# Halving the columns of the down projection's matmuls in the last eight tiles, and issuing them in runs of four

## The chip, the cores and the metric

The kernel runs on one core of a Trainium2 chip. The metric is the device time of one execution in microseconds (us), as the median over several runs. Engines are named as the profile names them: PE is TensorE's matmuls, PEld its weight loads, DVE VectorE, ACT ScalarE, POOL GpSimd, SP the queue that issues the DMAs.

## The reference

Two blocks follow each other. The first is a long convolution over the sequence, done with Fourier transforms. The second is an expert layer with a cosine gate, on each of the 49,920 rows that the first one gives. The change touches the second alone.

```python
# first block: x, v are (4, 12480, 128)
u = x * v
y = irfft(rfft(u, 2*S) * rfft(h_filt, 2*S))[:S]     # along the sequence
x2 = (x * y).reshape(49920, 128)
# second block: w_in (128, 2048), w_out (2048, 128)
h = x2 @ w_in
g = h * cos(h)
out = g @ w_out                                     # (49920, 128), float32
```

All is float32, in and out.

## The kernel before

The convolution is cut into steps that are mixed into the expert layer's loop for as long as there are any. Its last matmuls (line 504) start at 2945.7 us of the profiled execution; after that the expert layer runs alone. The prediction is about this last part.

**Tiles.** The 49,920 rows are taken four to a partition row: `G = 4`, so there are 12,480 groups of four. They form `NALL = 98` tiles: tile 0 with 104 groups (416 columns), tiles 1 to 96 with 128 (512 columns), tile 97 with 88 (352 columns). `NFC = 16` slices of 128 hidden features make the 16 steps of a tile. The loop over `steps` (lines 947 to 974) goes through all pairs of tile and slice; the variable `i` counts them.

**One step.** `moe_up` (740) multiplies a slice of `w_in` with the tile's rows into a bank `ph` of PSUM (PE, line 743). Then a chain of four engines forms h·cos(h). ACT scales `ph` and adds a quarter turn into `a` (746), DVE rounds `a` to `k` (749), POOL takes the difference `f` (752). `moe_act` (755) lets ACT take the sine of `f` into `cs` (757), and DVE multiplies it with `ph` into `gt` (759). `moe_down` (762) multiplies `gt` with a slice of `w_out` and sums it up over the 16 slices in one bank of PSUM, named `acc` for even tiles and `cv` for odd ones (PE, line 768).

**Order.** The engines run what they are given in the order in which the program gives it. In round `i` the loop issues the up projection of step `i` with its `a`, `k` and `f`, then the down projection of step `i - 4` (`LAG = 4`), after a tile's sixteenth down projection `moe_evict` (ACT, 774, the sums copied from PSUM into `ot`), and then `moe_act` of step `i - 1`, that is `cs` and `gt`. So on ACT the `cs` of one step stands behind the `a` of the next. After that come two visits of PE per tile that are transposes: `moe_turn` after the tile's step 3 turns the next tile's rows (four transposes at line 126, copied by ACT into `at` at 737), and `moe_back` at step 8 turns the finished sums of the tile before (four transposes, copied by ACT into `ob` at 783). `moe_store` (786) sends `ob` out by DMA.

**Banks.** `ph` is a ring of four PSUM banks (`ps_h`, line 910). `moe_up`, `moe_turn` and `moe_back` each take the next one, and it is free again when the last reader of its former content is done: `gt` for an up projection, the copies `at` and `ob` for the transposes. `a` has three buffers, `k`, `f` and `cs` two each, `gt` four, `ot` and `ob` one each.

**`slots`** (line 807) is the large SBUF tile of the convolution, 128 partitions of 64 x 240 x 2 values. It is not used after the convolution's end.

Of the kernel before, what the change touches and what calls it, by code (L numbers as in the profile page):

```python
# [9 lines left out]
F32 = mybir.dt.float32  # L10
# [6 lines left out]
P = 128  # L17
BANK = 512
# [12 lines left out]
def kernel(  # L31
# [46 lines left out]
    nc = tc.nc  # L78

    B, S, D = x.shape  # L80
    FO = pos_emb.shape[1]
    DFF = moe_w_in.shape[1]
    N1, N2 = 96, 120
# [15 lines left out]
    NFC = DFF // P  # L99
    G = BANK // D  # L100
    UA = 2
    NG = N2 // G
    NROWS = B * NG * R
    NALL = 1 + math.ceil((NROWS - R) / P)
    assert G == 2 * UA and H % UA == 0 and N2 % G == 0
    LAG = 4
    WCOL = 256

    dram = ctx.enter_context(tc.tile_pool(name="dram", bufs=1, space=DRAM))
# [14 lines left out]
    def transpose(dst, src, ident):  # L124
        n = src.shape[0]
        nc.tensor.transpose(dst, src, ident[0:n, 0:n])  # L126


    def float32_parts(pool, raw):
        lo, hi = raw[:, :, 0], raw[:, :, 1]  # L130

        power = pool.tile([P, WCOL], U32, name="power", bufs=2)
        nc.vector.tensor_scalar(out=power[:, :], in0=hi, scalar1=20, scalar2=0x7FF,
# [5 lines left out]

        sig = pool.tile([P, WCOL], U32, name="sig", bufs=2)  # L140
        nc.vector.tensor_scalar(out=sig[:, :], in0=hi, scalar1=0xFFFFF, scalar2=0x100000,
                                op0=ALU.bitwise_and, op1=ALU.bitwise_or)
        high = sig[:, :].bitcast(F32)
        nc.scalar.activation(high, sig[:, :], AF.Copy, scale=2.0 ** -20)
        low = pool.tile([P, WCOL], F32, name="low", bufs=1)
        nc.scalar.activation(low[:, :], lo, AF.Copy, scale=2.0 ** -52)
# [3 lines left out]
    def float32_join(dst, raw, power, high):  # L150
# [6 lines left out]
        if dst.space == DRAM:  # L157
# [3 lines left out]
    out_words = moe_w_out.bitcast(U32).rearrange("(c p) (q w) -> p c q w", p=P, w=2)  # L161
    in_pieces = [(slice(c, c + WCOL), in_words[:, c:c + WCOL, :])
                 for c in range(0, DFF, WCOL)]
    out_pieces = [(slice(c, c + WCOL // D), out_words[:, c:c + WCOL // D, :, :])
                  for c in range(0, NFC, WCOL // D)]
# [106 lines left out]
    def third_table(pool):  # L272

        return pool.tile([N2, 2, N2], F32, name="cs")
# [249 lines left out]
    made = [0]  # L524
# [191 lines left out]
    ats, accs = {}, {}  # L716

    def first_row(n):
        return min(R + (n - 1) * P, NROWS) if n else 0

    def rows_of(n):
        return first_row(n + 1) - first_row(n)
# [7 lines left out]
    def moe_turn(pool, n):  # L730
        m = rows_of(n)
        zb = zbs.pop(n)
        pt = ps_h.tile([P, BANK], F32, name="ph")
        for i in range(G):
            transpose(pt[:, i * m:(i + 1) * m], zb[0:m, i, :], ident)
        at = pool.tile([D, BANK], F32, name="at")
        nc.scalar.copy(out=at[:, 0:G * m], in_=pt[:, 0:G * m])
        ats[n] = at

    def moe_up(pool, n, c):  # L740
        m = G * rows_of(n)
        ph = ps_h.tile([P, BANK], F32, name="ph")
        nc.tensor.matmul(ph[:, 0:m], w_in_sb[:, c * P:(c + 1) * P], ats[n][:, 0:m],  # L743
                         start=True, stop=True)
        a = pool.tile([P, BANK], F32, name="a", bufs=3)
        nc.scalar.activation(a[:, 0:m], ph[:, 0:m], AF.Identity,  # L746
                             bias=quarter[:, 0:1], scale=INV_TWO_PI)
        k = pool.tile([P, BANK], F32, name="k")
        nc.vector.tensor_scalar(out=k[:, 0:m], in0=a[:, 0:m], scalar1=ROUND,  # L749
                                scalar2=ROUND, op0=ALU.add, op1=ALU.subtract)  # L750
        f = pool.tile([P, BANK], F32, name="f")
        nc.gpsimd.tensor_tensor(f[:, 0:m], a[:, 0:m], k[:, 0:m], op=ALU.subtract)  # L752
        return ph, f, m

    def moe_act(pool, ph, f, m):
        cs = pool.tile([P, BANK], F32, name="cs")
        nc.scalar.activation(cs[:, 0:m], f[:, 0:m], AF.Sin, scale=TWO_PI)  # L757
        gt = pool.tile([P, BANK], F32, name="gt", bufs=4)
        nc.vector.tensor_tensor(gt[:, 0:m], ph[:, 0:m], cs[:, 0:m], op=ALU.mult)  # L759
        return gt  # L760

    def moe_down(n, c, gt):
        if c == 0:

            accs[n] = bank() if made[0] == B * NG and n % 2 else \
                ps_acc.tile([P, BANK], F32, name="acc")
        m = G * rows_of(n)
        nc.tensor.matmul(accs[n][:, 0:m], w_out_sb[:, c, :], gt[:, 0:m],  # L768
                         start=(c == 0), stop=(c == NFC - 1))

    def moe_evict(pool, n):
        m = G * rows_of(n)
        ot = pool.tile([D, BANK], F32, name="ot", bufs=1)
        nc.scalar.copy(out=ot[:, 0:m], in_=accs.pop(n)[:, 0:m])
        return ot

    def moe_back(pool, n, ot):
        m = rows_of(n)
        pt = ps_h.tile([P, BANK], F32, name="ph")
        for i in range(G):  # L780
            transpose(pt[0:m, i * D:(i + 1) * D], ot[:, i * m:(i + 1) * m], ident)
        ob = pool.tile([P, 2, UA * D], F32, name="ob", bufs=1)
        nc.scalar.copy(out=ob[0:m, :, :].rearrange("p h n -> p (h n)"), in_=pt[0:m, :])
        return ob

    def moe_store(n, ob):
        row = first_row(n)
        while row < first_row(n + 1):
            b, g, n1 = row // R // NG, row // R % NG, row % R
            count = min(R - n1, first_row(n + 1) - row)  # L790
            first, _, second, _ = n2s(g)
            start = out[b * S + n1 * N2 + first, :]
            at = row - first_row(n)
            nc.sync.dma_start(
                bass.AP(tensor=start.tensor, offset=start.offset,
                        ap=[[N2 * D, count], [(second - first) * D, 2], [1, UA * D]]),
                ob[at:at + count, :, :])
            row += count

    with tc.manual_schedule():  # L800
        with tc.tile_pool(name="psum", bufs=8, space=PSUM) as psum, \
                ExitStack() as first:
            def bank():
                return psum.tile([P, BANK], F32, name="ps")

            spool = ctx.enter_context(tc.tile_pool(name="slots", bufs=1))
            slots = spool.tile([P, CB, 2 * N2, 2], F32, name="slots")
# [8 lines left out]
            with tc.tile_pool(name="layers", bufs=1, side="right") as pool:  # L816
# [14 lines left out]
                ident = pool.tile([P, P], F32, name="ident")  # L831
# [58 lines left out]
            cs = third_table(lpool)  # L890
# [9 lines left out]
            ident = wpool.tile([P, P], F32, name="ident")  # L900
            make_identity(nc, ident)
            w_in_sb = wpool.tile([D, DFF], F32, name="w_in_sb")
            w_out_sb = wpool.tile([P, NFC, D], F32, name="w_out_sb")
# [16 lines left out]
        mpool = ctx.enter_context(tc.tile_pool(name="moe", bufs=2))  # L920
# [18 lines left out]
        def load(n):  # L939
            while made[0] * R < first_row(n + 1):  # L940
                next(conv)
            moe_load(mpool, n)
# [3 lines left out]
        moe_turn(mpool, 0)  # L946
        steps = [(n, c) for n in range(NALL) for c in range(NFC)]
        hidden, gates, ots, obs = {}, {}, {}, {}
        for i in range(len(steps) + LAG):
            if i < len(steps):  # L950
                n, c = steps[i]
                if n == 0 and c == NFC // 2:
                    load(1)
                if c == NFC - 4 and n + 2 < NALL:
                    load(n + 2)
                hidden[i] = moe_up(mpool, n, c)
            if i >= LAG:
                pn, pc = steps[i - LAG]
                moe_down(pn, pc, gates.pop(i - LAG))
                if pc == NFC - 1:  # L960
                    ots[pn] = moe_evict(mpool, pn)
            if 0 <= i - 1 < len(steps):
                gates[i - 1] = moe_act(mpool, *hidden.pop(i - 1))
            if i < len(steps):

                if c == (LAG - 1 if n else NFC - 2) and n + 1 < NALL:
                    moe_turn(mpool, n + 1)
                if c == NFC // 2 and n - 1 in ots:
                    obs[n - 1] = moe_back(mpool, n - 1, ots.pop(n - 1))
                if c == NFC // 2 + 2 and n - 1 in obs:  # L970
                    moe_store(n - 1, obs.pop(n - 1))
            owed += 1.0
            while owed > 0.0:
                owed -= next(conv, owed)
        for n in sorted(ots):
            moe_store(n, moe_back(mpool, n, ots[n]))
# [28 lines left out]
```

## Time and profile before

| what | value |
|---|---|
| median of 3 runs | 3759.47 us (3757.68 to 3761.73) |
| span of the profiled execution | 3758.9 us |
| median less span (the profiled execution's own time is not listed apart from the runs) | 0.6 us |
| PE busy over the span | 98% |
| granted clock of PE, all 40 slices | 9 tenths or more |
| one 512-column tile with the convolution over (start to start) | 28.35 us |
| tile 90's first matmul, tile 97's first matmul | 3530.3 us, 3728.65 us |

A matmul of float32 values appears as two records of PE with a weight load before each. The end of a record is modelled; the distance from start to start is what a matmul costs when they follow each other. In the timeline "x2" joins the two records of one matmul, and the second number of a line is how long they take together, which is longer than the distance to the next matmul's start.

### The profile page before, as it was taken

The numbers are of one execution on the slowest core, as the hardware profiler recorded it, in microseconds if no ns is written. First come the engines' busy times: TensorE is split into PE (matmuls) and PEld (weight loads), VectorE is DVE, ScalarE is ACT, GpSimd is POOL, SyncE is SP. The second block draws the span as 40 slices with busy tenths as digits, with TensorE's granted clock in tenths as the row PEclk, the third lists the DMA queues.
The fourth block names the chain that finished last, engine by engine and source line by source line (L and its number), as shares of the span: only waits on it lengthen the run. The fifth ranks groups of instructions, "written<-read, shape, count | busy, mean of one in ns | idle before, by whom it ended". The sixth has DMA issues, their size and how long they took to land.

```text
span 3758.9 us, 47177 instructions
## 1 busy us (share of the span) xinstructions
PE 3690.6 (98%) x13546; PEld 2110.4 (56%) x13546; DVE 2773.7 (74%) x5586; ACT 2508.2 (67%) x4660; POOL 2557.6 (68%) x2318
## 2 busy tenths in 40 slices
PE   7898999999999999999999999999999999999999
PEld 6777555555566556555565556555566544444444
DVE  8887997687866787788766776788765666666666
ACT  5757776766665557766665567666664677777777
POOL 6666776588845665688745664788644677777776
PEclk9999999999999999999999999999999999999999
DMA  6263551022203650122104530122105200000000
GB/s 167 64 185 107 155 167 33 25 72 79 72 12 91 181 151 12 40 79 77 52 18 128 180 105 21 52 79 76 38 21 172 76 23 17 17 23 18 17 23 13
DMA packets 209499, 276.14 MB, mean 73 GB/s; under 512 B 17111, under 2 KB 146535, under 8 KB 209111
## 3 DMA queue, kind: packets, MB, share of 16 engines
q1 hardware_dynamic: 209239, 273.12, 24.8%
q8 instruction: 109, 1.79, 0.2%
q14 instruction: 151, 1.24, 0.1%
HBM read 193.64 MB, written 79.42 MB: 73 GB/s over the span
## 4 chain that ended last, share of the span: by engine, by line
PE 88%; DVE 3%; POOL 3%; ACT 2%; DMA 2%; issue 1%; SPq 0%; POOLq 0%; DVEq 0%; ACTq 0%
PE ph L743 33%; PE acc L768 28%; PE cv L504 5%; PE cv L768 5%; PE cv L479 4%; PE cv L407 3%; PE cv L448 3%; PE ph L126 2%; POOL f L752 1%; PE ps L407 1%; PE ps L448 1%; DMA tm<-td 1%; DMA wd<-w 1%; ACT cs L757 1%; DVE k L749 1%
## 5 line engine op out<-in xcount | busy, mean ns | idle before, releaser
L752 POOL TENSOR_TENSOR f<-a,k 128x512 f32<-128x512 f32 (+1 forms) x1568 | 1986.2, 1267 | 1060.5 <-DVE k L749 1059.1
L743 PE MATMUL ph<-at,w_in_sb 128*128 128x512 f32 (+1 forms) x3136 | 1599.0, 591 | 3.7 <-DVE gt L759 2.7
L746 ACT ACTIVATE a<-ph,quarter 128x512 f32<-128x512 f32 (+1 forms) x1568 | 1071.2, 683 | 704.8 <-PE ph L743 695.2
L768 PE MATMUL acc<-gt,w_out_sb 128*128 128x512 f32 (+1 forms) x2688 | 1370.3, 591 | 0.0
L759 DVE TENSOR_TENSOR gt<-ph,cs 128x512 f32<-128x512 f32 (+1 forms) x1568 | 1077.3, 687 | 359.9 <-ACT cs L757 341.8
L757 ACT ACTIVATE cs<-f 128x512 f32<-128x512 f32 (+1 forms) x1568 | 981.0, 626 | 366.6 <-POOL f L752 364.3
L749 DVE TENSOR_SCALAR k<-a 128x512 f32<-128x512 f32 (+1 forms) x1568 | 792.9, 506 | 550.7 <-ACT a L746 524.2
L768 PEld LDWEIGHTS acc<-gt,w_out_sb 128*128 128x128 f32 x2688 | 508.4, 189 | 642.8 <-issue 631.9
L743 PEld LDWEIGHTS ph<-at,w_in_sb 128*128 128x128 f32 x3136 | 553.2, 190 | 337.7 <-issue 257.5
L474 POOL TENSOR_TENSOR slots<-slots,t 120x256 f32<-120x256 f32 x384 | 312.9, 821 | 59.9 <-DVE t L467 25.6
L504 PEld LDWEIGHTS cv<-slots,tm 96*104 96x104 f32 x1920 | 238.6, 169 | 106.8 <-issue 85.4
L504 PE MATMUL cv<-slots,tm 96*104 96x128 f32 x1920 | 251.7, 273 | 9.9 <-POOL tm L297 5.0
L768 PE MATMUL cv<-gt,w_out_sb 128*128 128x512 f32 (+1 forms) x448 | 224.5, 583 | 1.0 <-DVE gt L759 1.0
L479 PEld LDWEIGHTS cv<-cs,slots 120*96 120x96 f32 x1536 | 176.7, 167 | 67.2 <-issue 65.2
L479 PE MATMUL cv<-cs,slots 120*96 120x120 f32 x1536 | 183.2, 266 | 0.0
L448 PEld LDWEIGHTS cv<-slots,w 124*120 124x120 f32 x576 | 103.7, 184 | 124.3 <-issue 112.3
L407 PEld LDWEIGHTS cv<-c,slots 104*124 104x124 f32 x768 | 132.6, 192 | 72.2 <-issue 60.0
L448 PE MATMUL cv<-slots,w 124*120 124x256 f32 x576 | 173.0, 380 | 0.0
L407 PE MATMUL cv<-c,slots 104*124 104x192 f32 x768 | 151.8, 327 | 5.4 <-DVE gt L759 3.5
L768 PEld LDWEIGHTS cv<-gt,w_out_sb 128*128 128x128 f32 x448 | 84.9, 190 | 104.8 <-issue 99.5
L489 DVE TENSOR_TENSOR slots<-cv,other 96x240 f32<-96x240 f32 x384 | 133.1, 394 | 1.5 <-ACT other L487 1.4
L395 DVE TENSOR_TENSOR xt<-xt,vt 104x256 f32<-104x256 f32 x177 | 132.6, 751 | 0.6 <-DMA vt<-in_v_dram 0.6
(131 smaller groups left out, 2520.9 us busy)
## 6 DMA issues: line engine op xcount, KB each, us to landing
h<-hd SPq DMA_DIRECT2D x144, 240.0 KB
tm<-td SPq DMA_DIRECT2D x96, 312.0 KB
xt<-in_x_dram SPq DMA_DIRECT2D x120, 208.0 KB
vt<-in_v_dram SPq DMA_DIRECT2D x120, 208.0 KB
xs<-in_x_dram SPq DMA_DIRECT2D x120, 208.0 KB
zd<-zs SPq DMA_DIRECT2D x119, 208.0 KB
zb<-zd SPq DMA_DIRECT2D x96, 256.0 KB
w<-wd SPq DMA_DIRECT2D x144, 116.2 KB
```

What stands on the lines that cost most here:

```text
L407: nc.tensor.matmul(ps[0:KE, i * 2 * N1:(i + 1) * 2 * N1], u[:, b, 0:KE, i], c1[0:u.shape[0], :, :].rearrange("p r k -> p (r k)"), start=Tr ...
L448: nc.tensor.matmul(pi, w[:, i, :], parts[0:KE, :, k], start=True, stop=True)
L474: nc.gpsimd.tensor_tensor(y[:, r], y[:, r], t[:, r], op=op)
L479: nc.tensor.matmul(ps[0:N1, (i * 2 + r) * N2:(i * 2 + r + 1) * N2], parts[0:N2, r, :, b, i], cs[:, r, :], start=True, stop=True)
L504: nc.tensor.matmul(ps[0:R, i * D:(i + 1) * D], t[:, i, r, :], slots[0:N1, :, place, :], start=(r == 0), stop=(r == 1))
L743: nc.tensor.matmul(ph[:, 0:m], w_in_sb[:, c * P:(c + 1) * P], ats[n][:, 0:m], start=True, stop=True)
L746: nc.scalar.activation(a[:, 0:m], ph[:, 0:m], AF.Identity, bias=quarter[:, 0:1], scale=INV_TWO_PI)
L749: nc.vector.tensor_scalar(out=k[:, 0:m], in0=a[:, 0:m], scalar1=ROUND, scalar2=ROUND, op0=ALU.add, op1=ALU.subtract)
L752: nc.gpsimd.tensor_tensor(f[:, 0:m], a[:, 0:m], k[:, 0:m], op=ALU.subtract)
L757: nc.scalar.activation(cs[:, 0:m], f[:, 0:m], AF.Sin, scale=TWO_PI)
L759: nc.vector.tensor_tensor(gt[:, 0:m], ph[:, 0:m], cs[:, 0:m], op=ALU.mult)
L768: nc.tensor.matmul(accs[n][:, 0:m], w_out_sb[:, c, :], gt[:, 0:m], start=(c == 0), stop=(c == NFC - 1))
```

## The change

From tile 90 on (`HALVED = NALL - 8`) each down projection is two matmuls instead of one: one with the first 64 columns of the `w_out` slice, which writes partitions 0 to 63 of the sums, and one with the other 64 columns, which writes partitions 64 to 127. Both read all of `gt`. These down projections are not issued in the round in which their step is due, but four at a time (`RUN = 4`), when the fourth of them is due. For that `gt` gets eight buffers, in a pool that is opened when tile 90's first `gt` is made, and `cs` is always taken from the same pool as before.

The last tile's sums are copied from PSUM not into `ot` but into `slots`, which is free by then: the value of column `c` of group member `i` lies at `240 c + i`, so the copy writes, and the four transposes then read, values that are 240 elements apart. 

```diff
+    RUN = 4
+    HALVED = NALL - 8
...
     def moe_act(pool, ph, f, m):
-        cs = pool.tile([P, BANK], F32, name="cs")
+        cs = mpool.tile([P, BANK], F32, name="cs")
...
-        gt = pool.tile([P, BANK], F32, name="gt", bufs=4)
+        gt = pool.tile([P, BANK], F32, name="gt", bufs=4 if pool is mpool else LAG + RUN)
...
     def moe_down(n, c, gt):
...
-        nc.tensor.matmul(accs[n][:, 0:m], w_out_sb[:, c, :], gt[:, 0:m],
-                         start=(c == 0), stop=(c == NFC - 1))
+        if n < HALVED:
+            nc.tensor.matmul(accs[n][:, 0:m], w_out_sb[:, c, :], gt[:, 0:m],
+                             start=(c == 0), stop=(c == NFC - 1))
+            return
+        for half in (slice(0, D // 2), slice(D // 2, D)):
+            nc.tensor.matmul(accs[n][half, 0:m], w_out_sb[:, c, half], gt[:, 0:m],
+                             start=(c == 0), stop=(c == NFC - 1))
...
     def moe_evict(pool, n):
         m = G * rows_of(n)
+        if n == NALL - 1:
+            apart = slots[:, :, :, :].rearrange("p b j i -> p (b j i)")
+            apart = apart[:, 0:m // G * 2 * N2].rearrange("p (c j) -> p j c", j=2 * N2)
+            ot = apart[:, 0:G, :]
+            nc.scalar.copy(out=ot, in_=accs.pop(n)[:, 0:m].rearrange("p (i c) -> p i c", i=G))
+            return ot
...
     def moe_back(pool, n, ot):
-            transpose(pt[0:m, i * D:(i + 1) * D], ot[:, i * m:(i + 1) * m], ident)
+            part = ot[:, i, :] if len(ot.shape) == 3 else ot[:, i * m:(i + 1) * m]
+            transpose(pt[0:m, i * D:(i + 1) * D], part, ident)
...
                 pn, pc = steps[i - LAG]
-                moe_down(pn, pc, gates.pop(i - LAG))
+                if pn < HALVED:
+                    moe_down(pn, pc, gates.pop(i - LAG))
+                elif pc % RUN == RUN - 1:
+                    for back in range(RUN - 1, -1, -1):
+                        moe_down(pn, pc - back, gates.pop(i - LAG - back))
                 if pc == NFC - 1:
                     ots[pn] = moe_evict(mpool, pn)
             if 0 <= i - 1 < len(steps):
-                gates[i - 1] = moe_act(mpool, *hidden.pop(i - 1))
+                if steps[i - 1] == (HALVED, 0):
+                    assert made[0] == B * NG
+                    ends.append(ctx.enter_context(tc.tile_pool(name="tail", bufs=1)))
+                gates[i - 1] = moe_act(ends[-1], *hidden.pop(i - 1))
```

## The prediction

> **What bounds the kernel now.** I read the busy shares of the page first, then busy times by stretch over the last tiles, then the timeline of one step, then the kernel's end. The page shows PE busy almost throughout, and the stretches show that this holds to the last tile:
>
> ```profile
> PE 3690.6 (98%) x13546; PEld 2110.4 (56%) x13546; DVE 2773.7 (74%) x5586; ACT 2508.2 (67%) x4660; POOL 2557.6 (68%) x2318
> ...
> PEclk9999999999999999999999999999999999999999
> ```
>
> ```profile
> core 0: us, PE busy (x) PEld busy (x) DVE busy (x) ACT busy (x) POOL busy (x), PEclk, DMA share, GB/s
> 3643.60:3671.95 28.35, 28.35 (x73) 12.94 (x72) 18.52 (x32) 22.02 (x36) 20.72 (x17) 1.00 0.07 19
> 3671.95:3700.30 28.35, 28.35 (x73) 12.94 (x72) 18.02 (x32) 22.20 (x36) 19.99 (x17) 1.00 0.05 16
> ...
> 3728.65:3758.90 30.25, 24.53 (x81) 13.97 (x79) 16.44 (x35) 18.56 (x39) 16.38 (x18) 1.00 0.06 15
> ```
>
> In a tile of 28.35 us PE never rests, at the full clock; ACT, next, has 6.2 us of slack and POOL 7.6. So the time of the last eight tiles is PE's work plus any wait that the change puts on PE. One step, followed through the four engines:
>
> ```profile
> 3720.07 1.02 PE L743 MATMUL ph<-at,w_in_sb 128*128 128x512 f32 x2
> 3720.93 1.02 PE L768 MATMUL acc<-gt,w_out_sb 128*128 128x512 f32 x2
> 3721.13 0.69 ACT L746 ACTIVATE a<-ph,quarter 128x512 f32<-128x512 f32 x1 [0.20 <-PE ph L743]
> 3721.78 1.02 PE L743 MATMUL ph<-at,w_in_sb 128*128 128x512 f32 x2
> 3721.92 0.43 DVE L749 TENSOR_SCALAR k<-a 128x512 f32<-128x512 f32 x1 [0.26 <-ACT a L746]
> 3722.42 1.27 POOL L752 TENSOR_TENSOR f<-a,k 128x512 f32<-128x512 f32 x1 [0.44 <-DVE k L749]
> 3723.73 0.63 ACT L757 ACTIVATE cs<-f 128x512 f32<-128x512 f32 x1 [0.20 <-POOL f L752]
> 3724.39 0.69 DVE L759 TENSOR_TENSOR gt<-ph,cs 128x512 f32<-128x512 f32 x1 [0.33 <-ACT cs L757]
> ```
>
> A projection takes 0.86 us from start to start, so one record 0.43, and its result comes 1.02 - 0.86 = 0.16 after PE is free for the next. From the end of an up projection to the end of its `gt` it is 3725.08 - 3721.09 = 4.0 us. The up projection that wants the same bank, four steps on, starts at 3720.07 + 4 x 1.716 = 3726.93, 5.8 us after the end of this one, and that hides the 4.0. Two more prices come from here:
>
> ```profile
> 3707.47 0.58 ACT L774 COPY ot<-cv 128x512 f32<-128x512 f32 x1 [0.17 <-PE cv L768]
> 3707.95 0.64 ACT L757 ACTIVATE cs<-f 128x512 f32<-128x512 f32 x1
> ...
> 3738.59 0.76 PE L768 MATMUL cv<-gt,w_out_sb 128*128 128x352 f32 x2
> ...
> 3751.66 0.86 PE L768 MATMUL cv<-gt,w_out_sb 128*128 128x352 f32 x2 [0.69 <-DVE gt L759]
> ```
>
> ACT instructions in a row overlap by 0.10. A matmul that had to wait for `gt` takes 0.10 to 0.11 more, because its weights were not loaded ahead, and it starts 0.05 after `gt` ends.
>
> **1. The new order: waits for a bank (+37).** PE's order becomes four ups, eight halves, four ups. Call E the moment when PE has streamed the first up of a run (step 4k+4). The ring of four makes the fourth up of that run wait for `gt` of step 4k+3, and that `gt` now starts late: its `cs` stands on ACT behind `a` of 4k+4, which needs the very up that stands behind the eight halves. From E: result 0.16, to ACT 0.04, `a` 0.69, overlap -0.10, `cs` 0.63, 0.04, `gt` 0.69, 0.05, weights 0.11: 2.31. Two ups take 1.72 meanwhile. PE waits 0.6 us. How long the halves take does not enter. This is the case of a tile's first and last run: 1.2.
> The run of steps 4 to 7 follows `moe_turn`, which takes a bank, so that step 5 waits for `gt` of 2 and step 6 for `gt` of 3. And `moe_evict` now stands on ACT behind the whole run of halves, with `cs` of 2 behind it. From D, the end of that run: evict starts at 0.20, `cs` of 2 ends at 1.31, `gt` at 2.04, step 5 can start at 2.20; PE was free at 0.44 (transposes) + 0.86 = 1.30, so 0.9 is lost. Then `at` to 1.78, `a` of 4 to 2.37, `cs` of 3 to 2.90, `gt` 3.63, step 6 at 3.79 against 3.06: 0.7. Sum 1.6.
> In steps 8 to 11 `moe_back` takes a bank after step 8: step 10 waits for `gt` of 7 (2.31 against 0.44 + 0.86 = 1.30: 1.0), step 11 for `gt` of 8, whose `cs` stands behind `ob` and `a` of 9: from E `f` of 8 ends at 2.77, `cs` 3.43, `gt` 4.16, start 4.32 against 3.17: 1.15. Sum 2.15.
> A tile loses 1.2 + 1.6 + 2.15 = 5.0 us; seven tiles 35, the last one, narrower and with no turn, about 2: 37. All of it is new, since PE waits nowhere in these tiles now.
>
> **2. The halves themselves.** No row has a matmul under 88 columns. The rows say that a record's time goes with the moving columns and not with the width of the weights: 591 ns for line 768 (512 moving, weights 128 wide) and 273 ns for line 504 (128 moving, 104 wide) both lie on 162 ns plus 0.84 to 0.87 ns a moving column. So a half takes 0.86 like a whole one. Bounds of a pair: 0.43, if a narrower matmul streams twice as fast and the halves run beside each other; 1.72, if one follows the other. I take 0.86, as in the row for line 768: the same weights, rows and sums on the same array, the two halves side by side.
> Within a half the two records still follow each other, so the second half begins with the second record of the first, and a run of four pairs takes nine records for eight: one record more a run, 28 runs x 0.43 + 4 runs x 0.30 = 13.
> The Trainium skill (TensorE: Matmul & The Clock Gate, Part 3) says that matmuls in different column groups run at once, measured for narrow ones at 2.38 times for three; no row here shows it, and it would make the pair 0.86.
>
> **3. Going from whole to half and back (+7).** Between no cost and a drained pipe plus an unhidden weight load, 0.16 + 0.11 = 0.27 each time; 64 times make 0 to 17. I take one unhidden load, the row at 3751.66: 64 x 0.11 = 7.
> The Trainium skill (TensorEngine Tiling, Key Properties) speaks against the change: going over to another tiling drains the engine. The trace has no such change; by the drained end the sum would be 10 us more.
>
> **4. Weight loads.** A pair has four loads where there were two. A load (0.19) is hidden by a record of 0.43; I cost it at nothing. If half of a pair's loads lost that cover, 128 pairs x 2 x 0.11 = 28.
>
> **5. The last tile's sums.** Evict, transposes and `ob` are on the path at the end (0.45, 0.64, 0.58 us). The nearest strided row is line 350, 480 values in pieces of eight, 480 elements apart, 0.57 us, as fast as contiguous copies (0.574 for 512). Single values may cost up to three times as much: 0 to 0.9 for the copy, 0 to 0.8 for the four loads. I take 0.3.
>
> **6. Edits at nothing.** `cs` has the pool it had. Opening the new pool and writing to `slots` wait for readers of the convolution, whose last matmul was at 2945.7, 585 us before tile 90. Eight `gt` buffers cover four waiting and four in work. The DMAs of a tile come later by its delay; they move 10 to 19 GB/s. `moe_evict`'s place is in part 1.
>
> **Sum.** 37 + 13 + 7 + 0.3 = 57 on the span of 3758.9: 3816; with the 0.6 that the median lies above it, 3817, +1.5%. With the bounds of parts 2 (no extra record) to 5 it is 3796 to 3828.
>
> **The rivals.**
> *One half after the other* (0.22). A second stream of `gt` into the array has no row, so it may not exist. Then each step pays 0.86 more: 7 x 16 x 0.86 + 16 x 0.59 = 106, part 1 stays, no extra record: 37 + 106 + 7 = 150, 3910 (3902 to 3920).
> *Side by side, with loads or reads in each other's way* (0.11): 28 (part 4) to 53 (half of the way to the rival above) more, 3845 to 3870.
> *Narrow matmuls stream faster* (0.07), the case on the other side. The place is the record of a half; at 0.21 instead of 0.43 a pair takes 0.43, PE saves 112 x 0.43 + 16 x 0.30 = 53 and pays the 37: -16; with tiles that short, POOL's and ACT's 20 to 22 us leave less slack and the waits grow, so I put it at -10: 3749. It decides from a pair of 0.86 - 5.0/16 = 0.55 down; for it speaks only that nothing measures it, against it every width in the trace.
> That the change does not do what it says is out: the program has four ups and eight 64-column matmuls in turn.
>
> **How the numbers follow.** The forecast gets 0.60. The range holds it, the second rival and the first one's lower part: 3792 to 3912, some 0.8. A measurement here can tell 0.2%, 7.5 us. Only the third rival can be faster by more, most of its chance: 0.05. Within 0.2%: the rest of it, and smaller waits with quicker halves: 0.05. Slower: 0.90.
>
> **What would show it.** Right: in tiles 90 to 96 the start-to-start time goes from 28.35 to about 36 us; PE's ups in the waits table wait for `gt`, some 5 us a tile, mostly at steps 5, 6, 10 and 11; a run of eight halves takes some 3.9 us; tiles before 90 are unchanged. Wrong: a run of some 7 us (first rival), or of under 2.5 (third), or ups that wait for nothing.

## The result, and the profile after

The changed kernel takes 3788.55 us (median of 4 runs) beside 3759.35 us for the kernel before: a ratio of 1.0078, 95% interval 1.0066 to 1.0090. It is slower by 29 us, half of the 57 that were forecast and 3.5 us below the range.

The page of the changed kernel, busy shares and granted clock:

```profile
PE 3710.7 (98%) x13802; PEld 2089.9 (55%) x13802; DVE 2784.8 (74%) x5586; ACT 2500.0 (66%) x4660; POOL 2562.0 (68%) x2318
...
PEclk9999999999999999999999999999999999999999
```

The whole page hides the change: PE is busy for 98% as before. The stretches of two of the halved tiles and of the end show it (same columns as before: length, then busy time of each engine):

```profile
3625.04:3657.24 32.20, 30.87 (x106) 10.36 (x104) 20.13 (x33) 20.78 (x35) 20.40 (x17) 1.00 0.06 17
3657.24:3689.45 32.21, 30.88 (x106) 10.36 (x104) 20.13 (x33) 20.79 (x35) 20.43 (x17) 1.00 0.06 18
3753.73:3786.90 33.17, 26.47 (x122) 11.48 (x120) 15.97 (x34) 17.88 (x37) 15.83 (x17) 0.97 0.05 14
```

A tile takes 32.20 us instead of 28.35, and from tile 97's first matmul to the end it is 3.0 us more than before. The forecast had 36 for a tile. PE's timeline of tile 92 (line 745 is the up projection, 775 the halves, 128 the transposes; "x6" joins six records, and the bracket is idle time and what ended it) shows where. A bracket is shorter than the wait, because the modelled end of the record before it lies 0.16 us behind the point at which the next could have started:

```profile
3592.84 2.84 PE L745 MATMUL ph<-at,w_in_sb 128*128 128x512 f32 x6
3595.99 1.13 PE L745 MATMUL ph<-at,w_in_sb 128*128 128x512 f32 x2 [0.30 <-DVE gt L761]
3597.04 3.65 PE L775 MATMUL cv<-gt,w_out_sb 128*64 128x512 f32 x16
3600.63 0.66 PE L128 MATMUL ph<-ident,zb 128*128 128x128 f32 x4
3601.12 1.02 PE L745 MATMUL ph<-at,w_in_sb 128*128 128x512 f32 x2
3602.39 2.96 PE L745 MATMUL ph<-at,w_in_sb 128*128 128x512 f32 x6 [0.24 <-ACT at L739]
3605.28 3.65 PE L775 MATMUL acc<-gt,w_out_sb 128*64 128x512 f32 x16
3608.86 1.12 PE L745 MATMUL ph<-at,w_in_sb 128*128 128x512 f32 x2
3609.82 0.60 PE L128 MATMUL ph<-ident,ot 128*128 128x128 f32 x4
3610.26 1.02 PE L745 MATMUL ph<-at,w_in_sb 128*128 128x512 f32 x2
3611.76 1.98 PE L745 MATMUL ph<-at,w_in_sb 128*128 128x512 f32 x4 [0.47 <-ACT ob L797]
3613.67 3.65 PE L775 MATMUL acc<-gt,w_out_sb 128*64 128x512 f32 x16
3617.26 2.84 PE L745 MATMUL ph<-at,w_in_sb 128*128 128x512 f32 x6
3620.40 1.12 PE L745 MATMUL ph<-at,w_in_sb 128*128 128x512 f32 x2 [0.31 <-DVE gt L761]
3621.46 3.65 PE L775 MATMUL acc<-gt,w_out_sb 128*64 128x512 f32 x16
```

Sixteen records of halves, 3597.04 to 3600.63, take 3.59 us. Eight whole records take 8 x 0.429 = 3.43. So the halves do run side by side, and there is no ninth record. From one part of PE's work to the next, less what the records need, the tile's 3.86 us more divide as follows ("step 3" is the up projection of the tile's slice 3, counted from 0):

- *Waits for banks, 2.51 us:* step 3 0.57, step 5 0.51, step 7 0.12, step 10 0.74, step 15 0.57. Each has 0.10 in it for the weight load that could not go ahead.
- *Into and out of the halves, 1.35 us, 0.34 a run:* 0.09 more before the run, 0.05 for its first weights, 0.10 after its last record, and 0.10 for the next up projection's first weights (0.06 where transposes come next).

From tile 90's start to the end of the span it is 257.7 us against 228.5 before, 29.1 more: 31 runs with up projections between them make 10.4 (less where transposes follow), the last tile's sums 0.33, and the rest, 18.4, are waits. (The tiles before 90 came 1.1 us earlier in this execution, which is why the spans differ by 28.0.)

The chain that ended last, over the same tile, passes through the other engines at each of these places:

```profile
3601.86 0.48 ACT at L739
3602.34 0.04 issue
3602.39 2.96 PE ph L745 x6
3605.35 3.58 PE acc L775 x16
...
3618.42 0.69 ACT a L748
3619.11 0.53 ACT cs L759
3619.64 0.02 issue
3619.66 0.70 DVE gt L761
3620.36 0.04 issue
3620.40 1.12 PE ph L745 x2
```

The lower half is part 1 of the prediction as it was written: `a` of one step, the `cs` of the step before behind it on ACT, `gt`, and only then the fourth up projection. The upper half is not: step 5 waits for `at`. That is the next tile's `at`, which step 5 does not read, so it is the bank that it waits for.

The last tile's sums, ACT's timeline at the end, before and after:

```profile
3753.76 0.45 ACT L774 COPY ot<-cv 128x352 f32<-128x352 f32 x1 [1.51 <-PE cv L768]
...
3781.52 0.75 ACT L784 COPY slots<-cv 128x352 f32<-128x352 f32 x1 [1.47 <-PE cv L775]
```

The copy takes 0.75 us instead of 0.45; the four transposes behind it 0.67 instead of 0.64.

### The profile page after: what moved, and what is told of

It reads as the page before. It is cut to its first block, busy times and chain, and to the rows that moved or that the text cites. A ratio compares the mean times of both kernels' runs of the same rounds, so it can differ in the third digit from the quotient of the medians.

```text
span 3786.9 us, 47683 instructions
## 1 busy us (share of the span) xinstructions
PE 3710.7 (98%) x13802; PEld 2089.9 (55%) x13802; DVE 2784.8 (74%) x5586; ACT 2500.0 (66%) x4660; POOL 2562.0 (68%) x2318
## 4 chain that ended last, share of the span: by engine, by line
PE 89%; DVE 3%; ACT 2%; POOL 2%; DMA 1%; issue 1%; SPq 0%; POOLq 0%; DVEq 0%; ACTq 0%
PE ph L745 33%; PE acc L771 27%; PE cv L506 5%; PE cv L481 4%; PE cv L771 4%; PE cv L450 3%; PE cv L409 3%; PE ph L128 2%; PE ps L409 2%; PE acc L775 2%; PE cv L775 1%; PE ps L450 1%; POOL f L754 1%; PE ps L481 1%; ACT cs L759 1%
## 5 line engine op out<-in xcount | busy, mean ns | idle before, releaser
L771 PE MATMUL acc<-gt,w_out_sb 128*128 128x512 f32 (+1 forms) x2560 | 1304.9, 591 | 0.0
L751 DVE TENSOR_SCALAR k<-a 128x512 f32<-128x512 f32 (+1 forms) x1568 | 810.5, 517 | 554.5 <-ACT a L748 531.8
L771 PEld LDWEIGHTS acc<-gt,w_out_sb 128*128 128x128 f32 x2560 | 484.0, 189 | 613.2 <-issue 602.9
L771 PE MATMUL cv<-gt,w_out_sb 128*128 128x512 f32 x320 | 163.4, 592 | 0.0
L473 DVE TENSOR_TENSOR slots<-cv,h 120x256 f32<-120x256 f32 x288 | 119.3, 414 | 0.0
```

## The experiments

All but one start from the changed kernel. Times are medians beside the kernel before on the same chip.

**Runs of four, but whole matmuls.** The order of issue alone.

```diff
-        if n < HALVED:
+        if n < NALL:
             nc.tensor.matmul(accs[n][:, 0:m], w_out_sb[:, c, :], gt[:, 0:m],
```

> The changed kernel, but the last eight tiles' down projections are whole 128-column matmuls again, still in runs of four. Theory A (from the two traces: the order of issue makes PE wait for PSUM banks, 2.5 us a tile, some 18 us; going into and out of the halves costs 0.32 us a run, 10.4 us; the strided sums 0.35): 18 + 0.35 above the kernel before, 3778. Rival B (the halves cost all of it, the runs nothing): 3760. Rival C (the prediction's plain ring of banks, 37 us of waits): 3797.

Measured: 3779.18 against 3760.23, ratio 1.0051 (1.0038 to 1.0064). 19 us of the 29 belong to the order of issue (with the 0.33 of the last tile's sums, which this kernel keeps) and none of them to the halves. In its trace a tile takes 31.0 us, with the waits at the same five steps.

**Two more banks.** Steps 3, 7, 11 and 15 and both visits of transposes take their bank from the pool of the odd tiles' sums.

```diff
-        ph = ps_h.tile([P, BANK], F32, name="ph")
+        ph = bank() if n >= HALVED and c % 4 == 3 else ps_h.tile([P, BANK], F32, name="ph")
...
-        pt = ps_h.tile([P, BANK], F32, name="ph")
+        pt = bank() if n >= HALVED else ps_h.tile([P, BANK], F32, name="ph")
```

(The second edit stands in `moe_back`; `moe_turn` has the same with `n > HALVED`.) With the halves:

> The changed kernel with two more PSUM banks for the last tiles: every fourth up projection and the two visits of transposes take theirs from the pool that holds the odd tiles' sums, where two of three banks are idle. Theory A: the waits for banks go, the price of going into and out of the halves stays: 10.4 + 0.35 above the kernel before, 3770. Rival B: banks do not matter, 3788 as the changed kernel.

Measured: 3770.41 against 3760.23, ratio 1.0028 (1.0018 to 1.0038). PE's timeline of a tile has no bracket left; what was ended by `gt`, `at` and `ob` is gone, and the time around the runs of sixteen is as it was:

```profile
3596.72 3.65 PE L775 MATMUL acc<-gt,w_out_sb 128*64 128x512 f32 x16
3600.30 1.13 PE L745 MATMUL ph<-at,w_in_sb 128*128 128x512 f32 x2
3601.27 0.60 PE L128 MATMUL cv<-ident,ot 128*128 128x128 f32 x4
3601.70 1.88 PE L745 MATMUL ph<-at,w_in_sb 128*128 128x512 f32 x4
3603.42 1.02 PE L745 MATMUL cv<-at,w_in_sb 128*128 128x512 f32 x2
3604.37 3.65 PE L775 MATMUL acc<-gt,w_out_sb 128*64 128x512 f32 x16
```

With whole matmuls:

> Both at once: runs of four whole matmuls, two more banks. Theory A: neither price is left but for the strided sums, 3760, as the kernel before. Were it above 3765, runs of four would cost something besides the banks (ACT's order, buffers of a, k, f, cs).

Measured: 3760.13 against 3760.23, ratio 1.0001 (0.9992 to 1.0010). The four kernels together show two prices that add up: the order of issue costs 19 us with four banks and nothing that can be told with six, the halves cost 10 either way. None of them is faster than the kernel before. In tiles 90 to 96 PE already worked without a rest there, and no record of a half is shorter than one of a whole matmul, so there was nothing to gain.

**The sine of the newest step ahead of the next `a`.**

```diff
-            if 0 <= i - 1 < len(steps):
+            due = [i - 1]
+            if i >= LAG and pn >= HALVED and pc % RUN == RUN - 1:
+                due.append(i)
+            for j in due:
+                if j not in hidden:
+                    continue
...
-                gates[i - 1] = moe_act(ends[-1], *hidden.pop(i - 1))
+                gates[j] = moe_act(ends[-1], *hidden.pop(j))
```

> The changed kernel, but right after each run of halves is issued, the sine and product of the newest step are issued too, so that they stand ahead of the next run's first a on ACT, not behind it. Theory A (the wait of 0.57 us at steps 3 and 15 is that place in ACT's queue): these two waits go, that at step 10 shrinks to about 0.25 us, that at step 5 grows to about 1.0 since the copy of the turned rows stands behind one more sine: 1.25 us a tile instead of 2.5, 9 us less than the changed kernel, 3779. Rival: the place on ACT does not matter, the chain of four engines is simply too long: 3788.

Measured: 3789.76 against 3760.23, ratio 1.0082 (1.0068 to 1.0095): no gain. The expectation missed. The wait at step 15 went, as did that at step 7, but step 3 waits 0.77 us, and steps 5, 6, 9 and 10 together 2.2: a tile of 32.63 us instead of 32.20. The start of a tile (its first up projection is at 3590.46):

```profile
3591.10 1.27 POOL L754 TENSOR_TENSOR f<-a,k 128x512 f32<-128x512 f32 x1 [0.36 <-DVE k L751]
...
3592.40 0.63 ACT L759 ACTIVATE cs<-f 128x512 f32<-128x512 f32 x1 [1.00 <-POOL f L754]
3592.94 1.25 ACT L748 ACTIVATE a<-ph,quarter 128x512 f32<-128x512 f32 x2
3593.06 0.69 DVE L761 TENSOR_TENSOR gt<-ph,cs 128x512 f32<-128x512 f32 x1 [0.94 <-ACT cs L759]
...
3593.81 0.70 PE L745 MATMUL ph<-at,w_in_sb 128*128 128x512 f32 x1 [0.51 <-DVE gt L761]
```

The sine now stands ahead, but ACT is idle for 1.0 us in front of it, because POOL ends the last `f` of the burst only at 3592.37; and the two `a` that used to be done by then stand behind it. So the place on ACT is what the chain shows in the changed kernel, but moving it moved the waits and did not lessen them. A likely reason, read from the trace and not tested by itself, is that four up projections in 3.4 us set off a chain that passes one step in about 1.64 us (the distance from `f` to `f` inside a burst, here 3589.46 and 3591.10), so that a `gt` comes late somewhere in the tile in either order. What is shown to help is another bank.

**Runs of one and of two.** `RUN = 1` and `RUN = 2` in place of 4.

> The changed kernel without runs: each step's two halves are issued when their step is due (RUN = 1, five buffers of gt). Theory A: no waits for banks, but 128 changes into and out of the halves at 0.335 us: 43 us above the kernel before, 3802. Rival (each change costs a drained pipe and an unhidden weight load, 0.27 each, as the upper bound of the prediction had it): 69 above, 3829. Rival (the halves are slower by themselves, however they are grouped): 3788 as the changed kernel.

Measured: 3801.19 against 3759.76, ratio 1.0109 (1.0094 to 1.0125), 41 us. The price goes with the number of changes in and out: 128 of them at 0.32 by the medians (0.34 in the trace of a tile).

> The changed kernel with runs of two (RUN = 2). Theory A: 64 changes in and out at 0.335 us, 21 us, and few waits for banks, since a bank is wanted again after two up projections and two pairs of halves, with the sine of two steps before not held up: 0 to 3 us; 3781 to 3784, less than the changed kernel. Rival (runs of any length bring the waits): 3795 or more.

Measured: 3785.09 against 3759.76, ratio 1.0066 (1.0054 to 1.0079), 25 us: 64 changes at 0.32 to 0.34 make 20 to 22, and the trace has one wait left, 0.5 us a tile at step 5, for `at`. This is 1 us above the range that was expected, no more than the runs of one kernel differ by.

**Four first halves, then four second halves.** Which order lets halves run beside each other.

```diff
-                    for back in range(RUN - 1, -1, -1):
-                        moe_down(pn, pc - back, gates.pop(i - LAG - back))
+                    for h in range(2):
+                        for back in range(RUN - 1, -1, -1):
+                            moe_down(pn, pc - back, gates[i - LAG - back], (h,))
```

> The changed kernel, but within a run the four first halves are issued first, then the four second halves. Theory A with matmuls started strictly in the order of the program: a first half finds only first halves beside it, and they follow each other on the same columns; only the last first half and the first second half can overlap: 15 records of 0.43 us a run instead of 8, 3.0 us more, 92 in all, 3880. Rival (PE looks ahead and pairs a second half with a first one of another step): 3788, as the changed kernel.

Measured: 3842.44 against 3759.76, ratio 1.0220 (1.0206 to 1.0234), between the two times expected. A run takes 5.35 us, twelve records. The weight loads of one run, by their start:

```profile
3600.99 0.19 PEld L775 LDWEIGHTS cv<-gt,w_out_sb 128*64 128x64 f32 x2 [0.76 <-issue]
3601.47 0.14 PEld L775 LDWEIGHTS cv<-gt,w_out_sb 128*64 128x64 f32 x1 [0.29 <-issue]
3601.90 0.14 PEld L775 LDWEIGHTS cv<-gt,w_out_sb 128*64 128x64 f32 x1 [0.29 <-issue]
3602.33 0.14 PEld L775 LDWEIGHTS cv<-gt,w_out_sb 128*64 128x64 f32 x1 [0.29 <-issue]
3602.76 0.19 PEld L775 LDWEIGHTS cv<-gt,w_out_sb 128*64 128x64 f32 x3 [0.29 <-issue]
```

For four records only first halves are at work. At 3602.76 three loads come together: as the third first half starts, the first second half starts too (its matmul record is at 3602.77), although the fourth first half, which stands ahead of it in the program, starts at 3603.62. So PE took a matmul ahead of its place, but not from the start of the run. Twelve records for eight make 4 x 0.43 x 28 runs + 4 x 0.30 x 4 = 53 us above the changed kernel's 29; 83 were measured.

**Two first, two second, in turn.** How far it looks.

```diff
-                    for h in range(2):
-                        for back in range(RUN - 1, -1, -1):
-                            moe_down(pn, pc - back, gates[i - LAG - back], (h,))
+                    for pair in ((3, 2), (1, 0)):
+                        for h in range(2):
+                            for back in pair:
+                                moe_down(pn, pc - back, gates[i - LAG - back], (h,))
```

> The changed kernel, but a run's eight halves in the order first, first, second, second, first, first, second, second. With four first halves ahead of the second ones, the first second half started together with the third first half, two matmuls ahead of its place, ahead of the fourth. Theory (PE looks two matmuls ahead, whatever the columns): the first second half starts with the first first half, every record has company, a run takes 3.6 us: 3788 as the changed kernel. Rival (it looks one matmul ahead): the first step's first half runs alone, ten records a run, 0.86 more, 26 in all: 3815. Rival (it was the end of two whole first halves that let the second one start, not a reach): 3815 or more.

Measured: 3792.33 against 3761.92, ratio 1.0079 (1.0062 to 1.0095). A run takes 3.63 us, as in the changed kernel but for 0.05, and its first two records start 13 ns apart:

```profile
3600.13 3.71 PE L775 MATMUL cv<-gt,w_out_sb 128*64 128x512 f32 x16
```

A half is started beside the half that stands two matmuls ahead of it; in the kernel with four first halves it was not started beside those that stood four and three ahead.

**One half left out.** The second half is computed in each tile's first step alone, so half of the last eight tiles' outputs lack the products of the other fifteen.

```diff
-        for half in (slice(0, D // 2), slice(D // 2, D)):
-            nc.tensor.matmul(accs[n][half, 0:m], w_out_sb[:, c, half], gt[:, 0:m],
+        if c == 0:
+            half = slice(D // 2, D)
+            nc.tensor.matmul(accs[n][half, 0:m], w_out_sb[:, c, half], gt[:, 0:m],
+                             start=True, stop=True)
+        half = slice(0, D // 2)
+        nc.tensor.matmul(accs[n][half, 0:m], w_out_sb[:, c, half], gt[:, 0:m],
```

> The changed kernel with the second half of the columns left out in all but each tile's first step, so that half of the outputs of the last eight tiles is not what the reference has. Theory (a half takes as long as a whole matmul, and the second one runs beside the first): leaving it out gains nothing, 3788. Rival (two halves share something, or a narrow matmul alone streams faster): less by up to 0.43 us a step, 53 in all, of which the waits for banks take back a part: 3745 to 3775.

Measured: 3790.65 against 3761.92, ratio 1.0075 (1.0060 to 1.0090). Eight records take as long as sixteen:

```profile
3599.24 3.65 PE L779 MATMUL cv<-gt,w_out_sb 128*64 128x512 f32 x8
```

The second half is free, and a half is not cheaper than a whole matmul.

**Sums at different distances.** The kernel before, with the copy of the sums spread as in the changed kernel's last tile.

```diff
+        step = {90: 4, 91: 8, 92: 16, 93: 60, 94: 120, 95: 240, 97: 240}.get(n)
+        if step:
+            ot = slots[:, :, :, :].rearrange("p b j i -> p (b j i)")[:, 0:m // G * step]
+            ot = ot.rearrange("p (c j) -> p j c", j=step)[:, 0:G, :]
```

> The kernel before with the sums of tiles 90 to 95 and 97 copied into the convolution's large tile 4, 8, 16, 60, 120, 240 and 240 elements apart, tile 96 as before. In the changed kernel the copy of 352 values took 0.746 us instead of 0.452, 0.84 ns more for each value. Theory: what costs is that no value has a neighbour, whatever the distance, so every copy of 512 values takes 0.58 + 0.43 = 1.0 us, and each transpose's weight load the same at each distance. Rival: the price grows with the distance, 4 apart costs nothing. The time stays within 1 us of the kernel before, since the copies are beside PE's work but for the last.

Measured: one run, 3761.24, inside the spread of the kernel before (3755.99 to 3764.43). ACT's copies of tiles 90 to 95, in order:

```profile
3564.86 1.10 ACT L777 COPY slots<-acc 128x512 f32<-128x512 f32 x1 [0.17 <-PE acc L768]
3593.43 1.10 ACT L777 COPY slots<-cv 128x512 f32<-128x512 f32 x1 [0.17 <-PE cv L768]
3621.99 1.04 ACT L777 COPY slots<-acc 128x512 f32<-128x512 f32 x1 [0.17 <-PE acc L768]
3650.48 1.10 ACT L777 COPY slots<-cv 128x512 f32<-128x512 f32 x1 [0.17 <-PE cv L768]
3679.04 1.12 ACT L777 COPY slots<-acc 128x512 f32<-128x512 f32 x1 [0.17 <-PE acc L768]
3707.61 1.04 ACT L777 COPY slots<-cv 128x512 f32<-128x512 f32 x1 [0.17 <-PE cv L768]
```

1.04 to 1.12 us at every distance from 4 to 240 elements, 0.58 where values are neighbours. The weight load of a transpose goes from 0.14 to 0.19 us.
The Trainium skill (SBUF — State Buffer, Specifications (TRN2)) has lines of 16 bytes, with a price for each access that crosses into another. Four float32 values fill such a line, and from a distance of four on the price here is full and grows no more, which agrees; distances of two and three were not run.

## Why the prediction was right or wrong

Right were the sign, the place (tiles 90 to 97 and nothing ahead of them), the two halves side by side, and the mechanism of part 1: with up projections in bursts PE waits for banks of PSUM. Of the 57 us, 29 came.

| part | predicted | measured |
|---|---|---|
| 1. waits for a bank | 37 | 18.4 in the trace, 19 by the runs of whole matmuls |
| 2. one record more in each run | 13 | 0 |
| 3. into and out of the halves | 7 (0.22 a run) | 10.4 (0.34 a run) |
| 5. last tile's sums | 0.3 | 0.33 |

**Part 1 failed at "a ring of four".** It let the transposes' bank lie idle for a whole turn of the ring, so that step 5 would wait for `gt` of 2, step 6 for `gt` of 3, step 11 for `gt` of 8. So had the account of the banks ahead of the prediction. In the program `ps_h` is four banks but no ring: the transposes' bank is handed to the second up projection after them, and step 5 waits for `at`, step 10 for `ob`, step 7 for `gt` of 3. By the prediction's own durations, step 5 could start 1.78 + 0.05 + 0.11 = 1.94 after the run's end, against 1.30: 0.64 (measured 0.51), and step 10, with `ob` done at 1.90, behind `a` of 8 and `cs` of 7, at 1.90 + 0.05 + 0.11 = 2.06 against 1.30: 0.76 (measured 0.74); step 7 would wait 0.13 (measured 0.12), steps 6 and 11 not at all. With 0.6 each at steps 3 and 15 that makes 2.7 us a tile where 5.0 were forecast and 2.5 measured. The waits at steps 3 and 15 were put at 0.6 and are 0.57. The trace of before had a line that spoke against the ring, in PE's weight loads after a turn:

```profile
3708.98 0.19 PEld L743 LDWEIGHTS ph<-at,w_in_sb 128*128 128x128 f32 x1 [0.32 <-ACT at L737]
```

This is the load for step 5 of the tile that began at 3700.40, and it starts 0.05 after the copy `at` ends: in a plain ring it would have had nothing to do with `at`.

**Part 1 also put too much on ACT's order.** The sum did not suffer, but in the kernel with the sine ahead only the waits at steps 15 and 7 went, others grew, and a tile got no shorter.

**Part 2 failed at "the second half begins with the second record of the first".** The records of the two halves start 7 ns apart, first with first and second with second, so a run needs eight. The kernels with other orders show that PE may start a matmul ahead of its place in the program, so the account of the order ahead of the prediction, by which every engine runs what it is given in the program's order, does not hold between halves. The Trainium skill (TensorE: Matmul & The Clock Gate, Part 3) has matmuls on different columns at work at once, which the trace confirms, and has them start and end strictly in the order of the program, which the run of four first and four second halves contradicts; here the measurement decides.

**Part 3 was too low by a third.** The one unhidden load is there on the way out (0.10), but besides it 0.09 are lost before the first half, 0.05 on its weights and 0.10 after the last one. The Trainium skill's rule that going over to another tiling drains the engine (TensorEngine Tiling, Key Properties) is in line with this, though no run here tells a drain from the other parts of the price; the measured price is 0.32 to 0.34 us for in and out together, inside the bounds that part 3 gave (0 to 0.54).

**Parts 4 to 6 held.** Weight loads stay hidden inside a run, the sums cost 0.33 us, and the edits costed at nothing left no wait in the trace. The bound of part 5, three times as much for values that are written singly, rested on no row; the copies took 1.65 (352 values) to 1.9 times as much (512).

The rivals: one half after the other is out (16 records in 3.59 us), and so are a faster narrow matmul (eight records of halves alone take as long) and two halves in each other's way (leaving one out gains nothing). That the forecast range began at 3792 came from taking 37 us of waits as certain: its lower end had bounds for parts 2 to 5 and none for part 1.

## What to carry to other kernels

Four matmuls issued in a burst need their results' banks back in a burst: count the banks, ask what each waits for, and look up which bank the allocator hands out, since a pool need not be a ring. Splitting a matmul's columns into two halves gained nothing here, where the whole matmul already used all 128 columns, and each change to halves and back cost about a third of a microsecond, so if it must be done, do it in long runs and with spare banks. A bound for a part that was walked through by hand is needed as much as for one that no row shows.

## What the runs showed of the hardware

- Two float32 matmuls of 64 columns each, on different columns, start 7 ns apart and take together as long as one of 128 columns (0.86 us at 512 moving columns).
- PE starts such a matmul beside the one that stands two places ahead of it in the program, past the one between them, and a run loses only 0.05 us by it (3.63 us for sixteen records). It does not start it beside those three and four places ahead: with four first halves in a row, four records run alone first (5.35 us).
- Going into and out of halves costs 0.32 to 0.34 us together, by runs of one (128 changes, 41 us) and of four (31 in the trace, 10.4 us).
- ACT's copy of 512 float32 values from PSUM takes 1.04 to 1.12 us when values are written 16 to 960 bytes apart, 0.58 when they are neighbours.
